# Attention: the second bank of a slot's logits for the maxima is asked for behind the filling products instead of together with the first

## The chip, the cores and the metric

One core of a Trainium2 chip runs one program: TensorE (PE, with its weight loads as PEld), VectorE (DVE), ScalarE (ACT), GpSimd (POOL) and SyncE (SP, which here issues nearly all transfers). The metric is the device time of one execution in microseconds (us). The kernel before takes 866.9 us, the median of three runs between 866.54 and 867.04.

## The reference

A transformer block on 2048 rows of 512 numbers, in float32:

```
h = layernorm(x) * (1 + ca) + sa
x = x + ga * A(h)          # attention, 32 heads of 16, 4 segments of 512 rows
h = layernorm(x) * (1 + cb) + sb
x = x + gb * ((h @ w_gate) * (h @ w_up)) @ w_down

A, per segment and head:
  p     = softmax(q k^T / 4 + mask)          # causal inside the segment
  a_dot = p v
  a_mem = phi(q) M / (phi(q) z + 1e-6)       # memory of the earlier segments
  o     = g * a_mem + (1 - g) * a_dot
  M, z += phi(k)^T v, sum phi(k)
```

The change touches how `softmax(q k^T)` is scheduled. Nothing that is computed changes.

## The kernel before

**Units.** Attention is cut into 32 units: a segment, a group of eight heads, and half of that group (four heads). A unit v runs through five slots, 0 to 4, in the loop near the end of the attention part. Each unit's logits are computed twice. First, with queries on the partitions, for the row maxima: `q_step(u, i)` (L284). It multiplies into two PSUM banks, `lq0` and `lq1`, each of which exists once, and VectorE reads each bank back with a custom masked minimum (`tensor_tensor_reduce`, shown as CUSTOM_DVE_ANT_0, followed by a short read of the accumulator) into a column of `nm`. Later, with keys on the partitions, for the exponentials: `k_step(v, slot)` (L319) multiplies into the two-bank tile `lk`, which also exists once, ScalarE takes `Exp` of both banks at once (L336), and GpSimd cuts the triangle (L342).

**What one slot contains, in program order.** The maxima's logits of a later unit (`q_step`, unit v+2 in slots 2 to 4, v+1 in slots 0 and 1); in slot 1 the products of the weights with the values of unit v-1 (`av_step`, tile `tb`, 32 products); in slot 4 the transposes of the unit before (`t_step`, tile `tr`, which VectorE turns into `rd` and `orow`); the filling products (`fill`, L1186: projections, memory products, layer norm transposes, each with their copies on ScalarE and their arithmetic on VectorE and GpSimd); and the keys' logits (`k_step`). Behind slot 2 stands `n_step(v+1)`: TensorE transposes `nm` (`ntp`), VectorE splits it into two bfloat16 rows (`nt`), and SP writes them into rows 96 and 97 of the queries, where `k_step(v+1, 0)` finds them some slots later.

**The shapes of `q_step`.** Step i = 0 and 2 (slots 2 and 4): one product of 512 columns per bank. Step 1 and 3 (slots 3 and 0): a product of 384 and one of 128 per bank. Step 4 (slot 1): two of 256 per bank.

**What sets the order.** TensorE's order is the program's: `MM` and `TP` chain every product to the one before. VectorE's order is the program's too, during attention (`vec.eng = CV`). The orders of ScalarE, GpSimd and SP are chosen by the scheduler of the framework, so they can move when the program is written in another order. A product into `lq0` or `lq1` has to wait until VectorE has reduced that bank for the last slot; one into `lk` until ScalarE has taken the exponential of the last slot.

**After attention** the feed-forward part runs with other pools; no line of it is touched.

Of the kernel before, what the change touches and what calls it, by code (L numbers as in the profile page):

```python
# [8 lines left out]
F32 = mybir.dt.float32  # L9
# [3 lines left out]
ALU = mybir.AluOpType  # L13
# [4 lines left out]
P = 128  # L18
S, D, H, DH, NSEG, L, F = 2048, 512, 32, 16, 4, 512, 1376
# [5 lines left out]
NEG = -3.0e38  # L25
# [32 lines left out]
def tile_kernel(ctx, tc, x, wq, wk_, wv, wo, beta, w_gate, w_up, w_down, c, w_mod, out):  # L58
# [4 lines left out]
    def open_pool(**kw):  # L63
        p = tc.tile_pool(**kw)
        return p, p.__enter__()
# [6 lines left out]
    def pe(i):  # L72

        if last_pe[0] is not None:
            tc.add_manual_dep(i.ins, last_pe[0].ins.name, NOSYNC, reason="order")
        last_pe[0] = i
        return i
# [6 lines left out]
    def MM(*a, **k):  # L84
        return pe(nc.tensor.matmul(*a, **k))  # L85
# [5 lines left out]
    vec, act = Switch(nc.vector), Switch(nc.scalar)  # L91
# [3 lines left out]
    psppool, psp = open_pool(name="psp", bufs=1, space=PSUM)  # L95
# [21 lines left out]
    def flush():  # L117

        while later:
            later.pop(0)()  # L120

    def rest_of():

        while soon:
            soon.pop(0)()
# [116 lines left out]
    def run(gen):  # L242
        try:
            while True:
                next(gen)
        except StopIteration as e:
            return e.value
# [10 lines left out]
    NQ = NSEG * NG * 2  # L258
    kst = [ap.tile([98, HQ, L], BF, name=f"kst{i}") for i in range(NB)]
    qst = [ap.tile([98, HQ, L], BF, name=f"qst{i}") for i in range(NB)]  # L260
    cmask = ap.tile([P, L], BF, name="cmask")
# [17 lines left out]

    nms = {}  # L280

    def q_step(u, i):

        Q, K = qst[u % NB], kst[u % NB]  # L284
        if i == 0:
            nms[u] = ap.tile([P, 16], F32, tag="nm", name=f"nm{u}", bufs=2)
        nm = nms[u]
        for b in range(2):
            h = i // 2 * 2 + b
            if i == 4:  # L290
                parts = ((2 * b, 1), (2 * b + 1, 1))
            else:
                parts = ((h, 3),) if i % 2 == 0 else ((h, 2), (h, 0))
            qp = psp.tile([P, L], F32, tag=f"lq{b}", name=f"q{u}_{i}_{b}", bufs=1)
            c = 0
            for hh, qb in parts:
                n = (qb + 1) * P
                MM(qp[:, c:c + n], Q[0:96, hh, qb * P:(qb + 1) * P], K[0:96, hh, 0:n], start=True, stop=True)
                c += n
            c = 0  # L300
            for hh, qb in parts:
                n = (qb + 1) * P
                vec.tensor_tensor_reduce(qp[:, c:c + n], qp[:, c:c + n], cmask[:, L - n:], -1.0, -NEG,
                                         ALU.add, ALU.min, nm[:, 4 * hh + qb:4 * hh + qb + 1])
                c += n

    def n_step(u):

# [37 lines left out]
    def av_step(u, kb):  # L346

        s, g, jq = u // 8, u // 2 % 4, u % 2
        if kb == 0:
            tbs[u] = pst([P, L], "tb", f"tb{u}", F32)  # L350
        n = L - kb * P
        for j in range(HQ):
            p, b = j // 2, j % 2
            hh = g * HG + jq * HQ + j
            if kb == 0:
                rhs, w = ptiles[u, p][:, b, :], sels[u, 1]
            elif kb == 2:
                rhs, w = ptiles[u, 4][:, p, 256 * b:256 * b + 256], sels[u, 4]
            else:
                c = 0 if kb == 1 else 384  # L360
                rhs, w = ptiles[u, 2 + p][:, b, c:c + n], sels[u, 3]
            x = MM(tbs[u][32 * j:32 * j + 32, kb * P:], vt[s % 2][kb][:, hh * VS:hh * VS + 32], rhs,
                   start=kb == 0, stop=kb == 2, tile_position=(0, 32 * j), skip_group_check=True)
            if j == 0:
                tc.add_manual_dep(x.ins, w.ins.name, SYNC, reason="all four heads")
        if kb == 2:
            tsbs[u] = ap.tile([P, L], F32, tag="tsb", name=f"tsb{u}", bufs=2)
            act.activation(tsbs[u], tbs.pop(u), AF.Copy)  # L368
# [140 lines left out]
    def wo_load(s, pool):  # L509
        rw = []  # L510
        for t in range(4):
            a = pool.tile([P, D], F32, tag="orl", name=f"orl{s}_{t}", bufs=4)
            n = D - P if s == NSEG - 1 else D
            pin(nc.sync.dma_start(a[:, 0:n], od[s][t][:, 0:n]))
            rw.append(a)
        return rw

    def wo_op(s, rw, us, gs=range(NG), stop=False):

        for g in gs:  # L520
            op = bank(f"op{s}_{g}", small=not stop)
            for t in range(4):
                a = rw[t][:, g * P:(g + 1) * P]
                if s == NSEG - 1 and g == NG - 1:
                    a = orows[NSEG * NG - 1][:, t].rearrange("p h e -> p (h e)")
                TP(op[:, t * P:(t + 1) * P], a, ident)
            nm = ("k", "q")[g % 2]
            i = s % 2 * 2 + g // 2
            oH = pw.tile([P, L], F32R, tag=f"w{nm}H{i}", name=f"oH{s}_{g}", bufs=1)
            oL = pw.tile([P, L], F32R, tag=f"w{nm}L{i}", name=f"oL{s}_{g}", bufs=1)  # L530
            ahead.append(act.activation(oH, op, AF.Copy))  # L531
            us.append((oH, oL))
            if stop:
                yield 0.45
                pin(vec.tensor_sub(oL, op, oH.bitcast(F32)))
            else:
                (soon if (s, g) in ((1, 0), (2, 1)) else later).append(lambda oL=oL, op=op, oH=oH: pin(vec.tensor_sub(oL, op, oH.bitcast(F32))))
                yield 0.45
            if stop and g % 2 == 1:
                yield False  # L540

    def xr_load(s, pool, tag="xr"):
        xrs = []
        for t in range(4):
            xr = pool.tile([P, D], F32, tag=tag, name=f"xr{s}_{t}", bufs=4)
            pin(nc.sync.dma_start(xr, x[rows(s, t), :]))
            xrs.append(xr)
        return xrs
# [546 lines left out]
    def until(*key):  # L1095
        while key not in done:
            credit[0] -= (mem_step() if len(key) == 3 and memq else next(fa)) or 0.0
# [52 lines left out]
    for v in range(-2, NQ + 1):  # L1150
        rate[0] = 5.5
        on, prev = 0 <= v < NQ, 0 <= v - 1 < NQ
        for slot in range(5):
            i = (slot + 3) % 5
            u = v + 2 if i < 3 else v + 1
            now[0] = slot
            if 0 <= u < NQ:
                q_step(u, i)
            if slot == 2:
                later.extend(after_n)  # L1160
                after_n.clear()
            flush()
            if prev and slot == 1:
                for kb in (0, 1, 3, 2):
                    av_step(v - 1, kb)
            if v == NQ and slot == 0:
                assert B["orl_free"]
                o3 = wo_load(3, wpool)
                xr3 = xr_load(3, B["pb"])
            if v == NQ and slot == 2:  # L1170
                for f in (fa, fb):
                    for _ in f:
                        pass
                btag[:] = ["ms", "sm", "ms"]
                us3 = []
                run(wo_op(3, o3, us3, range(NG - 1), True))
                lg1 = lnC(1, wpool, lambda: pc, wpool, "orl", 4, lambda name: dbank(name))
                next(lg1)
            if prev and slot == 4:
                if (v - 1) % 2 == 0 and v > 8:  # L1180
                    until((v - 1) // 8, (v - 1) // 2 % 4, 0)
                t_step(v - 1)
                if (v - 1) % 8 == 7:
                    osegs[0] += 1
            if slot == 2 and prev and (v - 1) % 8 == 7:
                vfree[0] = (v - 1) // 8 + 2  # L1186
            fill(share[slot], slot < 4)
            rest_of()
            if on:
                k_step(v, slot)  # L1190
            while behind:
                behind.pop(0)()
            if slot == 2 and 0 <= v + 1 < NQ:
                n_step(v + 1)
                if v + 3 < NQ:
                    load(v + 3)
            if slot == 1 and 3 <= v + 3 < NQ:
                until((v + 3) // 8, (v + 3) // 2 % 4)
# [91 lines left out]
    def dbank(name):  # L1290
        nd[0] += 1
        return pst((P, 512), ("lq0", "lk0", "lq1", "lk1")[nd[0] % 4], name)
# [310 lines left out]
    for n in range(NU):  # L1603
        p, nm, i = units[n]
# [69 lines left out]
```

## Time and profile before

| | |
|---|---|
| median of three runs | 866.9 us |
| profiled execution, its own time | 867.63 us |
| its span, first to last instruction | 865.9 us |
| attention slots, from the first exponential to the last | 55.2 to 494.5 us |
| busy: PE, DVE, ACT, POOL | 840.0, 648.3, 496.4, 273.9 us |
| granted TensorE clock, mean | 0.999 |

A timeline row gives start, duration, engine, line, operation and tiles; "x2" means that two instructions are merged into the row, and a bracket at the end gives the idle time of the engine before it and what ended it. In a row with groups the numbers behind the bar are busy us, the mean ns of one, and then the engine's idle time just before instructions of that group, with its releasers. Ends of products are modelled, so a product's row may reach beyond the start of the next one.

### The profile page before, as it was taken

The page shows a single profiled execution, that of the slowest core. Times are in us where ns is not written, and L with a number is a line of the kernel's source. Part 1 is how long each engine was busy: PE and PEld are TensorE (multiplying, and loading weights), DVE is VectorE, ACT ScalarE, POOL GpSimd, SP SyncE. Part 2 cuts the span into 40 slices and gives each one's busy share as a digit, 9 for nine tenths or more (in the row PEclk, how much of TensorE's full clock was granted, in tenths as well). Part 3 has the DMA queues.
Part 4 walks back from the last instruction along what each step waited for, and adds up shares of the span by engine and source line. Part 5 has one row for each costly group of instructions (what it writes and reads, how often), then busy time and mean ns, then how long its engine had stood idle before and what let it go on. Part 6 is the DMA issues. An engine that isn't in the chain of part 4 may idle for free.

```text
span 865.9 us, 14418 instructions
## 1 busy us (share of the span) xinstructions
PE 840.0 (97%) x4982; PEld 598.4 (69%) x4982; DVE 648.3 (75%) x1796; ACT 496.4 (57%) x759; POOL 273.9 (32%) x423
## 2 busy tenths in 40 slices
PE   9989999989999999999999999999999999999998
PEld 6755656555665656665666677788888778888876
DVE  6897767887778877688879457989987855446654
ACT  4758757677776785677545626344536546455230
POOL 2756536466546674575424610000000000000000
PEclk9999999999999999999999999999999999999999
DMA  8655434545526354557466348569561576335102
GB/s 268 141 165 146 120 102 123 154 138 157 152 76 189 112 147 123 128 157 238 127 225 195 114 160 266 207 209 341 197 232 50 196 265 213 153 134 182 32 18 97
DMA packets 83928, 139.57 MB, mean 161 GB/s; under 512 B 12720, under 2 KB 46768, under 8 KB 83856
## 3 DMA queue, kind: packets, MB, share of 16 engines
q1 hardware_dynamic: 83568, 138.52, 51.0%
q8 instruction: 39, 0.64, 0.3%
q14 instruction: 33, 0.27, 0.1%
q10 hardware_dynamic: 288, 0.15, 0.1%
HBM read 89.87 MB, written 48.50 MB: 160 GB/s over the span
## 4 chain that ended last, share of the span: by engine, by line
PE 80%; DVE 11%; ACT 6%; POOL 1%; issue 1%; DMA 1%; DVEq 0%; POOLq 0%; ACTq 0%
PE acc L1350 14%; PE tb L85 7%; PE Xg L1281 7%; PE Xu L1281 7%; PE k L85 6%; DVE q L39 6%; PE q L85 5%; PE vps L85 5%; PE wops L85 5%; PE Yu L1281 4%; PE Yg L1281 4%; PE kps L85 3%; PE qps L85 3%; ACT pt L336 2%; PE Zg L1281 1%; PE Zu L1281 1%
## 5 line engine op out<-in xcount | busy, mean ns | idle before, releaser
L39 DVE CUSTOM_DVE_ANT_0 q<-q,cmask 128x384 f32<-128x384 f32 (+3 forms) x512 | 245.6, 507 | 59.6 <-PE q L85 51.6
L336 ACT ACTIVATE pt<-k 128x1024 f32<-128x1024 f32 x160 | 163.8, 1024 | 65.0 <-PE k L85 64.6
L342 POOL TENSOR_SCALAR_AFFINE_SELECT pt<-pt 128x256 f32<-128x256 f32 (+1 forms) x224 | 97.4, 449 | 166.6 <-ACT pt L336 166.3
L85 PE MATMUL q<-kst,qst 96*128 96x384 bf16 (+3 forms) x512 | 103.3, 298 | 13.0 <-DVE nm L39 11.7
L85 PE MATMUL k<-qst,kst 98*128 98x384 bf16 (+3 forms) x512 | 97.1, 302 | 4.5 <-ACT pt L336 4.4
L1358 DVE TENSOR_TENSOR xa<-xa,acc 128x512 f32<-128x512 f32 x95 | 64.7, 682 | 39.8 <-PE acc L1350 38.0
L85 PE MATMUL tb<-pt,v 128*32 128x512 f32 (+3 forms) x1024 | 75.7, 436 | 0.0
L39 DVE DVE_READ_ACCUMULATOR2_ANT nm<- 128x1 f32 x512 | 71.7, 140 | 0.0
L85 PEld LDWEIGHTS <-kst 98*128 98x128 bf16 x512 | 37.8, 98 | 49.0 <-issue 43.0
L85 PEld LDWEIGHTS <-qst 96*128 96x128 bf16 x512 | 45.7, 97 | 35.7 <-issue 13.3
L1350 PE MATMUL acc<-dH,mH 128*128 128x512 f32 (+1 forms) x152 | 60.3, 397 | 0.0
L1350 PE MATMUL acc<-dL,mH 128*128 128x512 f32 (+1 forms) x152 | 60.1, 395 | 0.0
L1350 PE MATMUL acc<-dH,mL 128*128 128x512 f32 (+1 forms) x152 | 60.0, 394 | 0.0
L85 PEld LDWEIGHTS tb<-pt,v 128*32 128x32 f32 x1024 | 28.6, 109 | 38.8 <-issue 35.0
L368 ACT ACTIVATE tsb<-tb 128x512 f32<-128x512 f32 x32 | 19.0, 595 | 40.1 <-PE tb L85 40.1
L1350 PEld LDWEIGHTS acc<-dL,mH 128*128 128x128 f32 (+1 forms) x152 | 28.6, 188 | 7.1
L1350 PEld LDWEIGHTS acc<-dH,mL 128*128 128x128 f32 (+1 forms) x152 | 28.5, 188 | 7.1 <-DVE mL L1301 0.3
L1350 PEld LDWEIGHTS acc<-dH,mH 128*128 128x128 f32 (+1 forms) x152 | 28.5, 188 | 6.7
L85 PE MATMUL kps<-ahH,wkH 128*128 128x512 f32 x64 | 29.5, 461 | 0.0
L85 PE MATMUL wops<-woH,oH 128*128 128x512 f32 x64 | 28.2, 441 | 0.7 <-ACT oH L531 0.7
L85 PE MATMUL qps<-ahH,wqH 128*128 128x512 f32 x64 | 28.7, 448 | 0.0
L85 PE MATMUL vps<-wvH,ahH 128*128 128x512 f32 x64 | 28.3, 442 | 0.0
(399 smaller groups left out, 2021.4 us busy)
## 6 DMA issues: line engine op xcount, KB each, us to landing
wm<-in_w_mod_dram SPq DMA_DIRECT2D x24, 256.0 KB, 4.9
kd<-k SPq DMA_DIRECT2D x16, 384.0 KB, 2.9
qd<-q SPq DMA_DIRECT2D x16, 384.0 KB, 3.1
kst<-kd SPq DMA_DIRECT2D x32, 192.0 KB, 3.2
qst<-qd SPq DMA_DIRECT2D x32, 192.0 KB, 3.6
x<-in_x_dram SPq DMA_DIRECT2D x16, 256.0 KB, 4.5
kst<-kd SPq DMA_DIRECT2D x32, 128.0 KB, 3.1
qst<-qd SPq DMA_DIRECT2D x32, 128.0 KB, 3.5
```

The source lines that it names most:

```text
L39: i = getattr(self.eng, name)(*a, **k)
L85: return pe(nc.tensor.matmul(*a, **k))
L336: ex = act.activation(pt, kp, AF.Exp, scale=0.25)
L342: sels[u, i] = nc.gpsimd.affine_select(w, w, pattern=[[0, w.shape[1]], [1, P]], compare_op=ALU.is_ge, fill=0.0, base=0, channel_multiplier=-1)
L368: act.activation(tsbs[u], tbs.pop(u), AF.Copy)
L1281: pe(nc.tensor.matmul(ps[0:n], a, b[:, k], start=first and c == 0, stop=last and c == 5, skip_group_check=True))
L1350: pe(nc.tensor.matmul(ps, a[0:m, t * P:(t + 1) * P], b[0:m], start=j == 0, stop=j == n - 1))
L1358: vec.tensor_add(xa, xa, ps)
```

## The change

`q_step` becomes `q_half(u, i, b)`, which does one bank. At the head of the slot only bank 0 is asked for; bank 1 comes behind the filling products and ahead of the keys' logits.

```
-    def q_step(u, i):
+    def q_half(u, i, b):
...
-        if i == 0:
+        if i == b == 0:
             nms[u] = ap.tile([P, 16], F32, tag="nm", name=f"nm{u}", bufs=2)
...
-        for b in range(2):
-            h = i // 2 * 2 + b
...
+        h = i // 2 * 2 + b
...
             if 0 <= u < NQ:
-                q_step(u, i)
+                q_half(u, i, 0)
...
             fill(share[slot], slot < 4)
             rest_of()
+            if 0 <= u < NQ:
+                q_half(u, i, 1)
             if on:
                 k_step(v, slot)
```

No instruction is added or removed. What moves, at three places (the name q6_0_1 means unit 6, step 0, bank 1; vps are filling products for the values, k4_2 the keys' logits of unit 4 in slot 2).

TensorE in unit 4, slot 2, before:

```order
L85 LDWEIGHTS qst2_188
L85 MATMUL q6_0_0_1539<-kst2_184,qst2_188 128x512
L85 LDWEIGHTS qst2_188
L85 MATMUL q6_0_1_1542<-kst2_184,qst2_188 128x512
L85 MATMUL vps1_2_1547<-wvH0_264,ahH1_0_1066 128x512
L85 MATMUL vps1_2_1547<-wvH0_264,ahL1_0_1067 128x512
L85 MATMUL vps1_2_1547<-wvL0_265,ahH1_0_1066 128x512
L85 MATMUL vps1_2_1547<-wvH1_268,ahH1_1_1101 128x512
L85 MATMUL vps1_2_1547<-wvH1_268,ahL1_1_1102 128x512
L85 MATMUL vps1_2_1547<-wvL1_269,ahH1_1_1101 128x512
L85 LDWEIGHTS kst0_182
L85 MATMUL k4_2_1554<-qst0_186,kst0_182 128x384
```

and now:

```order
L85 LDWEIGHTS qst2_188
L85 MATMUL q6_0_0_1539<-kst2_184,qst2_188 128x512
L85 MATMUL vps1_2_1544<-wvH0_264,ahH1_0_1061 128x512
L85 MATMUL vps1_2_1544<-wvH0_264,ahL1_0_1062 128x512
L85 MATMUL vps1_2_1544<-wvL0_265,ahH1_0_1061 128x512
L85 MATMUL vps1_2_1544<-wvH1_268,ahH1_1_1098 128x512
L85 MATMUL vps1_2_1544<-wvH1_268,ahL1_1_1099 128x512
L85 MATMUL vps1_2_1544<-wvL1_269,ahH1_1_1098 128x512
L85 LDWEIGHTS qst2_188
L85 MATMUL q6_0_1_1551<-kst2_184,qst2_188 128x512
L85 LDWEIGHTS kst0_182
L85 MATMUL k4_2_1554<-qst0_186,kst0_182 128x384
```

The second bank's weight load and product went behind the six filling products; the filling products moved up by one product.

VectorE in unit 4, slot 4 (rd and orow belong to the transposes of the unit before), before:

```order
L39 ISA q6_2_0_1602,nm6_1538<-q6_2_0_1602,cmask_190 128x512
L39 ISA nm6_1538 128x1
L39 ISA q6_2_1_1605,nm6_1538<-q6_2_1_1605,cmask_190 128x512
L39 ISA nm6_1538 128x1
L39 RECIPROCAL rd3_1613<-tr3_1608 128x16
L39 TENSOR_TENSOR orow1_1452<-tr3_1608,rd3_1613 128x4x64
L39 ISA q6_3_0_1632,nm6_1538<-q6_3_0_1632,cmask_190 128x384
```

and now:

```order
L39 ISA q6_2_0_1602,nm6_1538<-q6_2_0_1602,cmask_190 128x512
L39 ISA nm6_1538 128x1
L39 RECIPROCAL rd3_1610<-tr3_1605 128x16
L39 TENSOR_TENSOR orow1_1449<-tr3_1605,rd3_1610 128x4x64
L39 ISA q6_2_1_1621,nm6_1538<-q6_2_1_1621,cmask_190 128x512
L39 ISA nm6_1538 128x1
L39 ISA q6_3_0_1632,nm6_1538<-q6_3_0_1632,cmask_190 128x384
```

The slot's other VectorE work now stands ahead of the second bank's reduction.

ScalarE in unit 7, slots 2 and 3 (pt7_2 and pt7_3 are the exponentials of these slots; kf, k3, rlk and phk work up a projection of the keys that a filling product has finished), before:

```order
L820 ACTIVATE kf1_2_2084<-kps1_2_1991 128x512
L336 ACTIVATE pt7_2_2099<-k7_2_2094 128x1024
L824 ACTIVATE k3_1_2_2086<-kf1_2_2084 128x512
L848 ACTIVATE rlk1_2_2091<-kf1_2_2084 128x512
L848 ACTIVATE phk1_2_2090<-kf1_2_2084 128x512
L907 ACTIVATE us1_1_2076<-up1_1_1_2126 128x272
L336 ACTIVATE pt7_3_2143<-k7_3_2138 128x1024
```

and now:

```order
L819 ACTIVATE kf1_2_2081<-kps1_2_1988 128x512
L823 ACTIVATE k3_1_2_2083<-kf1_2_2081 128x512
L847 ACTIVATE rlk1_2_2088<-kf1_2_2081 128x512
L847 ACTIVATE phk1_2_2087<-kf1_2_2081 128x512
L335 ACTIVATE pt7_2_2099<-k7_2_2094 128x1024
L906 ACTIVATE us1_1_2073<-up1_1_1_2121 128x272
L827 CAST k3_1_2_2083<-kr_1_2_2084 128x512
```

The scheduler put the exponential of slot 2 behind the three copies that had followed it. The same happens at ten exponentials of the 160: at pt2_3, pt6_3, pt7_2, pt8_3, pt10_3, pt11_2, pt15_3, pt16_2, pt19_3 and pt23_3. Other single swaps on ScalarE, GpSimd and SP are there too, none of them by more than two places.

More of the change, by code (lines that the diff above doesn't have):

```diff
@@ L280, in tile_kernel @@
     nms = {}
-    def q_step(u, i):
+    def q_half(u, i, b):
         Q, K = qst[u % NB], kst[u % NB]
-        if i == 0:
+        if i == b == 0:
             nms[u] = ap.tile([P, 16], F32, tag="nm", name=f"nm{u}", bufs=2)
         nm = nms[u]
-        for b in range(2):
-            h = i // 2 * 2 + b
[L290 to L305, printed above, removed]
+        h = i // 2 * 2 + b
+        if i == 4:
+            parts = ((2 * b, 1), (2 * b + 1, 1))
+        else:
+            parts = ((h, 3),) if i % 2 == 0 else ((h, 2), (h, 0))
+        qp = psp.tile([P, L], F32, tag=f"lq{b}", name=f"q{u}_{i}_{b}", bufs=1)
+        c = 0
+        for hh, qb in parts:
+            n = (qb + 1) * P
+            MM(qp[:, c:c + n], Q[0:96, hh, qb * P:(qb + 1) * P], K[0:96, hh, 0:n], start=True, stop=True)
+            c += n
+        c = 0
+        for hh, qb in parts:
+            n = (qb + 1) * P
+            vec.tensor_tensor_reduce(qp[:, c:c + n], qp[:, c:c + n], cmask[:, L - n:], -1.0, -NEG,
+                                     ALU.add, ALU.min, nm[:, 4 * hh + qb:4 * hh + qb + 1])
+            c += n
     def n_step(u):
```

## The prediction

> **What bounds the kernel now.** I read the page's busy shares first, then the table of busy time by stretch, then the groups of TensorE rows with shapes kept apart, then single slots in the timeline, and the chain of waits between them.
>
> ```profile
> PE 840.0 (97%) x4982; PEld 598.4 (69%) x4982; DVE 648.3 (75%) x1796; ACT 496.4 (57%) x759; POOL 273.9 (32%) x423
> 200.00:250.00 50.00, 49.40 (x347) 32.30 (x345) 39.24 (x140) 33.84 (x47) 26.36 (x40) 1.00 0.46 124
> 550.00:600.00 50.00, 50.00 (x217) 40.49 (x217) 46.39 (x86) 22.45 (x41) 0.00 (x0) 1.00 0.70 244
> L85 PE MATMUL q<-kst,qst 96*128 96x512 bf16 x128 | 42.6, 379 | 7.2 <-DVE nm L39 7.0
> L85 PE MATMUL q<-kst,qst 96*128 96x384 bf16 x128 | 35.2, 326 | 0.4 <-DVE nm L39 0.4
> L85 PE MATMUL q<-kst,qst 96*128 96x256 bf16 x128 | 21.8, 271 | 5.3 <-DVE nm L39 4.2 <-DVE den L39 0.5
>   DVE nm L39: 11.7, 30
>   DVE den L39: 0.5, 1
> ```
>
> In the two rows of stretches the columns behind the length are PE, PEld, DVE, ACT, POOL. TensorE is the bound in both stages; the feed-forward stretch has no idle at all, so what attention gains or loses passes through to the end. In attention (200 to 250) VectorE is busy 39.2 of 50 and ScalarE 33.8: neither is the bound on average, both are close enough to be late in single slots. The waits that the change can touch are the next three rows: 7.2 us ahead of the 512-column products (slots 2 and 4), 5.3 ahead of the 256-column ones (slot 1), 0.4 ahead of the others, 12.9 in all, in some 31 waits.
>
> These 12.9 are too few. One regular stretch of unit 4, VectorE and then TensorE:
>
> ```profile
> 112.92 0.70 DVE L39 CUSTOM_DVE_ANT_0 q<-q,cmask 128x512 f32<-128x512 f32 x1 [1.34 <-PE q L85]
> ...
> 113.54 0.73 DVE L39 CUSTOM_DVE_ANT_0 q<-q,cmask 128x512 f32<-128x512 f32 x1
> 114.19 0.14 DVE L39 DVE_READ_ACCUMULATOR2_ANT nm<- 128x1 f32 x1
> 115.10 0.28 DVE L39 CAST nt<-ntp 16x128 bf16<-16x128 f32 x1 [0.77 <-PE ntp L88]
> ...
> 115.63 0.54 DVE L39 CUSTOM_DVE_ANT_0 q<-q,cmask 128x384 f32<-128x384 f32 x1
> ...
> 116.48 0.60 DVE L39 CUSTOM_DVE_ANT_0 q<-q,cmask 128x384 f32<-128x384 f32 x1
> ...
> 117.39 0.14 DVE L39 DVE_READ_ACCUMULATOR2_ANT nm<- 128x1 f32 x1
> ...
> 112.50 0.60 PE L85 MATMUL q<-kst,qst 96*128 96x512 bf16 x2
> ...
> 114.34 0.61 PE L85 MATMUL k<-qst,kst 98*128 98x384 bf16 x4
> 114.79 0.28 PE L88 MATMUL ntp<-ident,nm 128*16 128x128 f32 x1
> 114.90 0.60 PE L85 MATMUL q<-kst,qst 96*128 96x384 bf16 x4
> ...
> 116.79 0.61 PE L85 MATMUL k<-qst,kst 98*128 98x384 bf16 x4
> 117.24 0.72 PE L85 MATMUL q<-kst,qst 96*128 96x512 bf16 x2
> 117.80 0.38 PE L88 MATMUL tr<-ident,tsb 128*128 128x128 f32 x2
> ```
>
> Two undisturbed 512-column products make a row of 0.60 (112.50); at 117.24 the same two make 0.72, with no idle shown. The second one did wait 0.12, because VectorE finished the second bank of slot 3 only at 117.53 (117.39 + 0.14); the wait is swallowed by the modelled end of the first (0.38 mean, of which 0.60 - 0.38 = 0.22 is the real pitch). So each wait that is shown is short by about 0.16, and those under 0.16 don't show. With 31 waits that is 12.9 + 5.0 = 17.9 at most; I take **17 us** as what TensorE loses to these waits, split like the shown idle: 9.5 at 512 columns, 7.0 at 256, 0.5 at the rest. The Trainium skill (Perfetto Trace Analysis, section Tensor Engine Instruction) says that a product's reported end is an estimate from its size and not observed; the trace agrees with the 0.72 against 0.60. Taken without that, the sum would start from 12.9.
>
> **The change, part by part.** No product, reduction or transfer is added: 160 weight-and-product groups move within a slot, and every wait on a bank stays, only at another place.
>
> *Seams.* Before, a slot has one passage from filling products to bfloat16 logits (filling to k) and one back (q to filling). It still has one of each (filling to second q, first q to filling): 0.
>
> *Slot 3 into slot 4 (most of the 9.5).* Before, VectorE has to do nt and both banks of slot 3 before TensorE can go past the second product of slot 4: 115.63 to 117.53 is 1.90 for the banks. Now the second product of slot 2 stands ahead of k: at 114.34 - 0.22 = 114.1 (the filling products came up by 0.22, the k logits stay). Its reduction takes 0.42 to start (112.50 to 112.92) and lasts 0.79 (113.54 to 114.33), to 115.3. nt follows, 0.53, to 115.8 instead of 115.63; then one bank of slot 3, 0.95, to 116.8. That is what the first product of slot 4 needs at 117.24: 0.4 to spare where 0.12 was missing. So waits up to about 0.5 vanish and longer ones shrink by that much. Bounds: all 9.5 gone, or only the short half of them. The long ones have other VectorE work ahead of nt, which stays. I take two thirds: **-6.3** (between -4 and -9.5).
>
> *Slot 0 into slot 1 (the 7.0).* Here the chain of waits shows what is late:
>
> ```profile
> 90.37 0.48 ACT kf L820
> 90.86 1.02 ACT pt L336
> 91.88 0.52 ACT k L824
> 92.40 0.52 ACT rlk L848
> 92.92 0.53 ACT phk L848
> 93.47 0.92 DVE phk L39
> 94.39 0.47 DVE q L39
> 95.31 0.46 DVE q L39
> ```
>
> A finished projection goes through kf, an exponential, k3, rlk and phk on ScalarE, then phk on VectorE; both banks of slot 0 stand behind it (94.39 to about 96.2). Now phk is followed by the second bank of slot 4 and the first bank of slot 0: again two reductions, 0.79 + 0.95 against 1.9, and wanted 0.22 earlier, by the first product of slot 1 instead of the second. That is no relief at all. The gain is only that phk comes earlier: by 0.22, since the filling products ended earlier, and by an exponential (1.02) at places where the exponential now stands behind it. Bounds 0 and -7.0; I take a third, **-2.3**.
>
> *The exponentials.* ScalarE's order moved with the program. Unit 7:
>
> ```profile
> 157.21 0.40 PE L85 MATMUL kps<-ahL,wkH 128*128 128x512 f32 x1
> 157.44 0.61 PE L85 MATMUL k<-qst,kst 98*128 98x384 bf16 x4
> 159.66 0.61 PE L85 MATMUL k<-qst,kst 98*128 98x384 bf16 x4
> 157.64 0.60 ACT L820 ACTIVATE kf<-kps 128x512 f32<-128x512 f32 x1 [0.30 <-PE kps L85]
> 158.13 1.02 ACT L336 ACTIVATE pt<-k 128x1024 f32<-128x1024 f32 x1
> 159.03 0.63 ACT L824 ACTIVATE k<-kf 128x512 bf16<-128x512 f32 x1
> 159.56 0.63 ACT L848 ACTIVATE rlk<-kf 128x512 f32<-128x512 f32 x1
> 160.08 0.63 ACT L848 ACTIVATE phk<-kf 128x512 f32<-128x512 f32 x1
> 160.60 0.39 ACT L907 ACTIVATE us<-up 128x272 f32<-128x272 f32 x1
> 160.87 1.03 ACT L336 ACTIVATE pt<-k 128x1024 f32<-128x1024 f32 x1
> ```
>
> Now kf starts at 157.64 - 0.22 = 157.42; k3, rlk and phk follow at 0.49 and then 0.52 each, so the exponential starts at 159.47 instead of 158.13 and ends at 160.4. The next keys' logits, due at 159.66 into the same tile, wait about **0.8**. Three of the ten moved exponentials stand ahead of slot 3 (pt7_2, pt11_2, pt16_2). From k to k that slot lasted 2.22 here (157.44 to 159.66), but 2.45 with six filling products (114.34 to 116.79), so at the other two I put 0.5. The seven others stand ahead of slot 4, longer by the four transposes (two make the row at 117.80, 0.38): 0 to 0.4, and 0.25 as a rule. Sum 0.8 + 2 x 0.5 + 7 x 0.25 = **+3.5**. Bounds: 0, where VectorE's lateness covers it, and ten times 0.8. The ScalarE queue is what hurts here: the row at 160.87 shows an exponential that starts 1.21 after its first product (159.66), right behind the us that precedes it. The Trainium skill (TensorE: Matmul & The Clock Gate, section on the array being 16 pieces of 32x32) gives the queues of ScalarE and VectorE as strictly first in, first out; the trace agrees with that 1.21, and by the rule each of the ten waits for all three copies, ready or not. It is the mechanism of the slower rival below.
>
> *New waits.* The second product, and k behind it, now stand behind whatever the slot's VectorE work delays. The bank has a whole slot for that, so I price it from 0 to one reduction (0.79) at four places, 3: **+0.5**. nt is 0.2 later than before; the transfer that follows is wanted in slot 0 of the next unit, two slots of 2.4 and 2.8 later: 0. SP's loads behind it are wanted a unit later: 0.
>
> Sum: -6.3 - 2.3 + 3.5 + 0.5 = **-4.6**. The profiled execution is 867.63 (span 865.9 and 1.7 around it), 0.7 above the median of the runs; 866.9 - 4.6 = **862.3 us**.
>
> **The rivals.**
>
> *The exponentials decide (slower).* At all ten places the next keys' logits wait 0.8, +8, because the products ahead of them no longer wait for VectorE and so arrive sooner at `lk`; the relief of slot 4 is at its lower bound, -4, and slot 1 gives nothing: +4, **870.9**. For it: the rows above, where 1.34 us of delay meet a slack of 0.54. Against it: seven of the ten stand ahead of a long slot, and the phk that goes first is the one that slot 1 waits for. It decides once the exponentials cost more than slot 4 gives.
>
> *The waits move and nothing is left.* VectorE does the same reductions in the same pairs, only 0.2 to 0.8 earlier in a slot, and wants them 0.2 earlier; as in slot 1, slot 4 gets no more than the 0.12 of the regular slots, 0.12 at half of the 32 units, 1.9, and the exponentials take it: **866.9**. For it: phk, not the banks, is what is late at 93.47. Against it: 115.63 to 117.53, where nothing but the two banks is late.
>
> *Nearly all goes.* The 9.5 vanish, the early phk takes most of the 7.0 (-5), and the exponentials cost 2 where VectorE was late anyway: -12.5, **854.4**. For it: VectorE has 11 of 50 us idle. Against it: the waits of over 0.5 hang on ScalarE.
>
> **How the numbers follow.** The forecast, a gain of 2 to 9 us, has 0.52; nearly all gone 0.12; nothing left 0.12; slower 0.24. What a measurement can tell from no change is 0.2%, 1.7 us. Faster is 0.52 + 0.12 = 0.64, same 0.12, slower 0.24. The likeliest case's own range is 858 to 865; to leave out no more than two in ten I go down into the fastest case, 855, and up to the slower one, 871.
>
> **What would show it.** Right: the idle ahead of the 512-column products falls from 7.2 to 2 or less, the one ahead of the 256-column products stays above 3, and the idle ahead of k, fed by ScalarE, grows by about 3. The pair at 112.50 comes apart, and the row 117.24 has no hidden wait. Wrong: the 512-column products still wait for nm; or the keys' logits wait over 8 us for the exponential; or filling products begin to wait for VectorE, which no row here shows and for which I have no price.

## The result, and the profile after

The changed kernel takes 860.26 us (median of six runs, 859.71 to 862.23) against 866.96 us for the kernel before on the same chip (six runs): a ratio of 0.9926, 95% interval 0.9913 to 0.9938. It is faster by 6.7 us; 862.3 was forecast. Its profiled execution was its longest, 862.23 us with a span of 860.5: in it the granted clock stood at 0.50 from 137.35 to 140.76, right after TensorE's longest wait in the attention slots (1.64 us, ended at 136.49). The 32 `tb` products there took 3.75 us; 32 of them at 209.01 took 2.36. Half of 3.41 us is about 1.7 us, an estimate of what this cost; the other five runs had mean clocks of 0.999 to 1.0.

First the TensorE groups with shapes kept apart, after (behind the last bar stands the idle time just before a group and what ended it; other groups stand between these rows). The exponential, L336 before, is L335 now, and L343 in one experiment:

```profile
L85 PE MATMUL q<-kst,qst 96*128 96x512 bf16 x128 | 49.2, 384 | 2.7 <-DVE nm L39 1.5 <-DMA qd<-q 0.5
L85 PE MATMUL q<-kst,qst 96*128 96x384 bf16 x128 | 42.4, 331 | 3.3 <-DVE nm L39 3.2
L85 PE MATMUL q<-kst,qst 96*128 96x256 bf16 x128 | 24.8, 275 | 1.6 <-DVE nm L39 1.2
L85 PE MATMUL k<-qst,kst 98*128 98x512 bf16 x128 | 38.2, 379 | 0.6 <-ACT pt L335 0.6
L85 PE MATMUL k<-qst,kst 98*128 98x384 bf16 x128 | 34.9, 326 | 2.5 <-ACT pt L335 2.3
L85 PE MATMUL k<-qst,kst 98*128 98x256 bf16 x128 | 19.2, 271 | 2.6 <-ACT pt L335 2.4
```

and the keys' logits in the kernel before:

```profile
L85 PE MATMUL k<-qst,kst 98*128 98x512 bf16 x128 | 38.6, 383 | 1.8 <-ACT pt L336 1.8
L85 PE MATMUL k<-qst,kst 98*128 98x384 bf16 x128 | 35.4, 330 | 2.6 <-ACT pt L336 2.6
L85 PE MATMUL k<-qst,kst 98*128 98x256 bf16 x128 | 19.5, 275 | 0.1
```

The idle time ahead of q, most of it waits for VectorE, fell at 512 and at 256 columns, from 7.2 and 5.3 to 2.7 and 1.6, and rose at 384, from 0.4 to 3.3. The idle time ahead of k, nearly all of it waits for ScalarE's exponentials, moved: at 512 columns down by 1.2, at 256 columns up by 2.5.

Idle time is too small a number here, because a product's modelled end covers the first 0.16 us of every wait. So I also took the starts of the products: start to start, less the tenth percentile of the same pair of neighbours in the same trace, everything over 0.06 us summed from the first of the maxima's products (at 36.6 us) to the end of the attention slots. By that measure TensorE lost 22.0 us ahead of q and 5.2 ahead of k before, and 12.5 and 8.9 after. The sum fell from 27.2 to 21.4, 5.8 us. The two profiled executions differ by 867.63 - 862.23 = 5.4, or about 7.1 without the stretch at half clock, and the medians by 6.7. The table under the experiments has the same numbers for all of them, and what the measure leaves out stands below it.

The regular stretch of unit 4 that the prediction worked through, after the change:

```profile
113.97 0.70 DVE L39 CUSTOM_DVE_ANT_0 q<-q,cmask 128x512 f32<-128x512 f32 x1 [0.62 <-PE q L85]
...
114.58 0.27 DVE L39 CAST nt<-ntp 16x128 bf16<-16x128 f32 x1
...
115.10 0.54 DVE L39 CUSTOM_DVE_ANT_0 q<-q,cmask 128x384 f32<-128x384 f32 x1
...
115.95 0.14 DVE L39 DVE_READ_ACCUMULATOR2_ANT nm<- 128x1 f32 x1
116.42 0.57 DVE L39 CUSTOM_DVE_ANT_0 q<-q,cmask 128x384 f32<-128x384 f32 x1 [0.33 <-PE q L85]
...
113.54 0.39 PE L85 MATMUL q<-kst,qst 96*128 96x512 bf16 x1
...
114.32 0.38 PE L85 MATMUL q<-kst,qst 96*128 96x384 bf16 x2
...
115.99 0.39 PE L85 MATMUL q<-kst,qst 96*128 96x384 bf16 x2
...
116.66 0.38 PE L85 MATMUL q<-kst,qst 96*128 96x512 bf16 x1
```

nt now runs right behind the second bank of slot 2, one bank of slot 3 is reduced by 116.09 (115.95 + 0.14), and the first product of slot 4, at 116.66, finds it free with 0.6 to spare. Before, the second product of that slot was 0.12 late.

And ScalarE with TensorE in unit 10, at one of the ten moved exponentials, after the change:

```profile
203.15 0.60 ACT L819 ACTIVATE kf<-kps 128x512 f32<-128x512 f32 x1 [0.94 <-PE kps L85]
203.78 0.63 ACT L823 ACTIVATE k<-kf 128x512 bf16<-128x512 f32 x1
204.31 0.62 ACT L847 ACTIVATE rlk<-kf 128x512 f32<-128x512 f32 x1
204.84 0.61 ACT L847 ACTIVATE phk<-kf 128x512 f32<-128x512 f32 x1
205.35 1.00 ACT L335 ACTIVATE pt<-k 128x1024 f32<-128x1024 f32 x1
...
203.18 0.60 PE L85 MATMUL k<-qst,kst 98*128 98x384 bf16 x4
...
206.41 0.60 PE L85 MATMUL k<-qst,kst 98*128 98x256 bf16 x4 [0.34 <-ACT pt L335]
```

The logits of slot 3 were begun at 203.18, their exponential starts 2.2 us later, behind three copies, and the logits of slot 4 wait for it.

### The profile page after: what moved, and what is told of

The parts are those of the page before. It is cut to its first block, busy times and chain, and to the rows that moved or that the text cites. A ratio compares the mean times of both kernels' runs of the same rounds, so it can differ in the third digit from the quotient of the medians.

```text
span 860.5 us, 14421 instructions
## 1 busy us (share of the span) xinstructions
PE 839.1 (98%) x4982; PEld 599.1 (70%) x4982; DVE 643.1 (75%) x1796; ACT 499.1 (58%) x759; POOL 275.8 (32%) x423
## 4 chain that ended last, share of the span: by engine, by line
PE 84%; ACT 7%; DVE 6%; issue 1%; POOL 0%; DMA 0%; DVEq 0%; ACTq 0%
PE acc L1351 14%; PE tb L85 8%; PE Xg L1282 7%; PE Xu L1282 7%; PE k L85 6%; PE q L85 6%; PE wops L85 5%; PE vps L85 5%; PE kps L85 4%; PE Yu L1282 4%; PE Yg L1282 4%; DVE q L39 3%; PE qps L85 3%; ACT pt L335 2%; PE Zg L1282 1%; PE Zu L1282 1%
## 5 line engine op out<-in xcount | busy, mean ns | idle before, releaser
L335 ACT ACTIVATE pt<-k 128x1024 f32<-128x1024 f32 x160 | 163.9, 1024 | 76.9 <-PE k L85 75.0
L85 PE MATMUL q<-kst,qst 96*128 96x384 bf16 (+3 forms) x512 | 123.0, 302 | 7.6 <-DVE nm L39 6.0
L85 PEld LDWEIGHTS <-kst 98*128 98x128 bf16 x512 | 44.5, 97 | 30.2 <-issue 15.2
```

The source lines that it names most:

```text
L335: ex = act.activation(pt, kp, AF.Exp, scale=0.25)
```

## The experiments

**1. The change with the exponentials put back.** At the ten places the copies are tied behind the exponential; the order on TensorE and VectorE is that of the change. The trace shows that the scheduler answered with a move of its own: three other exponentials (pt3_0, pt8_0 and pt16_4), which stand ahead of three copies both before and in the change, come behind them here.

```
...
+        for c in copies[TEN[u, i]] if (u, i) in TEN else ():
+            tc.add_manual_dep(c.ins, ex.ins.name, NOSYNC, reason="order")
```

> The changed kernel, with the exponential put back ahead of the copies (k3 or q3, rl, ph) at the ten places where the scheduler had moved it behind them. My theory: relief of the waits on VectorE and the late exponentials are two effects that add up; the changed kernel waits some 5.9 us ahead of the keys' logits at the ten places (0.3 to 1.0 each, from its timeline), and these go, of which up to 2 come back ahead of the 256-column products, because phk is later again: 855 to 858 us. Rival: the early phk is what the change lives on; then the waits of slot 1 come back in full and the time is 861 to 866.

862.02 us, ratio 0.9950 (0.9936 to 0.9963): slower than the change by 1.8 us (only the change's longest run, the one with the stretch at half clock, reaches into the range of these), not faster by 2 to 5. The waits ahead of k did fall, from 8.9 to 3.8 us, and those ahead of q rose by more, from 12.5 to 18.9. The place is visible in unit 10, VectorE and then TensorE:

```profile
205.23 0.98 DVE L39 SCALAR_TENSOR_TENSOR phk<-phk,rlk 128x512 f32<-128x512 f32 x1 [0.82 <-ACT phk L850]
206.13 0.68 DVE L39 CUSTOM_DVE_ANT_0 q<-q,cmask 128x512 f32<-128x512 f32 x1
...
206.74 0.59 DVE L39 CUSTOM_DVE_ANT_0 q<-q,cmask 128x384 f32<-128x384 f32 x1
...
204.47 0.39 PE L85 MATMUL q<-kst,qst 96*128 96x512 bf16 x1
...
206.93 0.38 PE L85 MATMUL q<-kst,qst 96*128 96x384 bf16 x2 [0.42 <-DVE nm L39]
```

The second bank of slot 4 was written at 204.47. VectorE had nothing else to do, stood 0.82 us in front of phk waiting for ScalarE, and reduced the bank only at 206.13; the second product of slot 0 wants that bank and waits until 206.93. So the rival held in its number and in its mechanism, that the early phk pays for the late exponentials, but not in its place: in slot 1 the waits came back by 2.5 of 5.9, and as much more, 3.5, came at the 384-column products. How much of the 1.8 us the three other exponentials make, this run does not separate.

**2. The kernel before with the exponentials late.** Only ScalarE's order is changed, at the same ten places.

```
...
+        if (u, i) in TEN:
+            tc.add_manual_dep(ex.ins, copies[TEN[u, i]].ins.name, NOSYNC, reason="order")
```

> The kernel before (both banks together), with the exponential put behind the third copy at the same ten places. My theory: the exponentials come late there too, and only the part of the waits on VectorE that hangs on phk is given back: 867 to 872 us. Rival (the change lives on the early phk): 861 to 864 with both banks still together.

868.10 us, ratio 1.0013 (1.0004 to 1.0022), inside the range of the theory and outside the rival's. ScalarE's new order alone is worth nothing, rather a loss of 1.1 us: waits ahead of k rise by 6.6, those ahead of q fall by 5.4. The split without the ten (experiment 1 against before, with its three other late exponentials) is worth 5.0 us, both together 6.7.

**3 and 4. The second bank late in some slots only:** in 1 and 4, or, with (0, 2, 3) in both lines, in the others.

```
+                if slot not in (1, 4):
+                    q_half(u, i, 1)
...
-            if 0 <= u < NQ:
+            if 0 <= u < NQ and slot in (1, 4):
                 q_half(u, i, 1)
```

> Second bank behind the filling products in slots 1 and 4 alone, together with the first in slots 0, 2 and 3; the ten exponentials then stand where they stood before the change. My theory: a wait of slot 4 is a wait of its second product for the second bank of slot 3 (and slot 1 for slot 0); moving these two alone is enough, and the early reductions of slots 0, 2 and 3 keep VectorE ahead: 855 to 859 us, idle ahead of the 512- and 256-column products under 3 us together, idle ahead of k as before (4.5). Rival (spreading in every slot is what helps): two fifths of the gain, 863 to 865.

> The opposite: second bank behind the filling products in slots 0, 2 and 3, together with the first in slots 1 and 4. My theory: now the second product of slots 4 and 1 wants a bank that was handed to VectorE only some 0.7 to 0.9 us earlier, while a reduction takes about 0.4 to start and 0.8 to 1.0 to run: 0.4 to 0.7 us lost at each of 64 places, and the ten exponentials stay late: 885 to 905 us. Rival (spreading helps slot by slot): between the two kernels, 862 to 866.

Slots 1 and 4: 897.38 us, ratio 1.0348 (1.0331 to 1.0365), both theories wrong. Slots 0, 2 and 3: 912.94 us, 1.0531 (1.0517 to 1.0545), somewhat beyond my range. What I had counted for the second variant holds for the first as well: wherever a slot with a late second bank is followed by one with an early second bank, the bank is asked for twice within one k and one q. Both variants have two such passages in a unit. Slot 1 into slot 2 of a unit, TensorE and then VectorE, with late banks in slots 1 and 4:

```profile
117.34 0.39 PE L85 MATMUL q<-kst,qst 96*128 96x256 bf16 x2
...
118.01 0.38 PE L85 MATMUL q<-kst,qst 96*128 96x512 bf16 x1
118.84 0.38 PE L85 MATMUL q<-kst,qst 96*128 96x512 bf16 x1 [0.45 <-DVE nm L39]
...
117.77 0.43 DVE L39 CUSTOM_DVE_ANT_0 q<-q,cmask 128x256 f32<-128x256 f32 x1 [1.60 <-PE q L85]
...
118.65 0.14 DVE L39 DVE_READ_ACCUMULATOR2_ANT nm<- 128x1 f32 x1
```

The bank is written at 117.34, freed at 118.79, and wanted at 118.01 + 0.22. By the starts, the passage from slot 1 to slot 2 loses about 0.62 us in 31 of the 32 units, and the one from slot 4 to slot 0 loses 30 us in all. Over the two kernels that is (897.4 - 867.0) / 64 = 0.47 and (912.9 - 867.0) / 64 = 0.72 us a passage, net of all else; in it are two and three stretches of 3.41 us with a granted clock of 0.50, by the estimate above some 3.4 and 5.1 us. So the split helps only where every slot has it; the share of single slots can't be had this way.

**5 to 7. phk behind the second bank.** `feature2`, which puts phk (and phq, the same for a projection of the queries) on VectorE, is held back until the second bank's reduction has been issued; in the kernel before, until the filling products are done. `release` issues what is held back.

```
-                later.append(feature2)
+                (later if fast else heldback).append(feature2)
...
                 q_half(u, i, 1)
+            release()
```

> The changed kernel, with phk (and phq) of a filling projection put behind the second bank's reduction on VectorE instead of ahead of it; ScalarE's order stays. My theory now: what is left of the waits on VectorE is the second bank (and the first bank behind it) standing behind a phk that ScalarE has not delivered; about half of the 12 us that the starts of the products still show goes: 854 to 858 us, the 3.3 of idle ahead of the 384-column products falls under 1. Rival: the work is late by its amount and not by its place; then the wait only moves to the next bank and the time is 859.5 to 861.

> The same move in the kernel before: phk behind the filling products' other VectorE work, both banks still together at the head of the slot, ScalarE's order as before. My theory: there both banks of the slot stand ahead of phk already, and the two of the next slot behind it as before; phk is ready at the latest by then, so little changes: 865.5 to 868 us. Rival (a late phk alone is the whole matter, the split does nothing): as fast as the changed kernel with the same move, under 861.

> The changed kernel with both: the ten exponentials ahead of the copies, and phk behind the second bank's reduction. My theory: the trade between late exponentials and a late phk is undone, so the waits ahead of k fall by the 5 us that the exponentials alone gave back and the waits on VectorE do not rise again: 852 to 857 us, the fastest of all. Rival: phk is then so late that the memory products wait for it, or the next slot's first bank does: 859 to 863.

On the change: 858.66 us, ratio 0.9900 (0.9885 to 0.9916), between the two ranges, nearer to the theory's 858 than to the rival's 859.5; the 384-column idle fell from 3.3 to 1.2, not under 1. On the kernel before: 866.18 us, 0.9992 (0.9984 to 1.0001), as expected; there the edit moves hardly anything (phk or phq at four places, by one or two). On the change with the exponentials first: **856.41 us**, 0.9875 (0.9862 to 0.9889), in its range and the fastest of all, 10.6 us under the kernel before and 3.9 under the change. The three other exponentials of experiment 1 stand in their old place here. Against experiment 5 the waits ahead of k fell by 5.9, and those ahead of q rose by 3.1, which the expectation had not foreseen. Its groups on TensorE:

```profile
L85 PE MATMUL q<-kst,qst 96*128 96x512 bf16 x128 | 49.2, 384 | 4.2 <-DVE nm L39 3.4 <-DMA qd<-q 0.5
L85 PE MATMUL q<-kst,qst 96*128 96x384 bf16 x128 | 42.4, 331 | 1.3 <-DVE nm L39 1.2
L85 PE MATMUL q<-kst,qst 96*128 96x256 bf16 x128 | 24.6, 273 | 3.1 <-DVE nm L39 2.8
L85 PE MATMUL k<-qst,kst 98*128 98x384 bf16 x128 | 34.9, 326 | 0.6 <-ACT pt L343 0.3
```

and the row of VectorE's waits for phk (us in all, how many, the longest), from experiment 1 and from this kernel:

```profile
DVE phk L39 <- ACT phk L850: 8.1, 8, 2.4
...
DVE phk L39 <- ACT phk L857: 2.5, 3, 1.1
```

In experiment 5, with the ten exponentials still late, the row has 2.6 in 3 waits. Putting the exponentials first costs 1.8 us while phk stands ahead of the bank (with three others late), and brings 2.3 us (858.66 to 856.41) once it stands behind it.

All of them by the starts of the products, in us (medians, waits lost ahead of q by columns, and ahead of k):

| | median | q 512 | q 384 | q 256 | k |
|---|---|---|---|---|---|
| before | 867.0 | 12.2 | 1.0 | 8.7 | 5.2 |
| the change | 860.3 | 5.3 | 4.4 | 2.8 | 8.9 |
| 1: exponentials put back | 862.0 | 5.8 | 7.9 | 5.3 | 3.8 |
| 2: before, exponentials late | 868.1 | 10.4 | 1.2 | 4.9 | 11.8 |
| 5: phk behind | 858.7 | 5.8 | 1.8 | 3.0 | 9.3 |
| 6: before, phk behind | 866.2 | 12.2 | 1.1 | 7.8 | 5.3 |
| 7: phk behind, exponentials first | 856.4 | 6.9 | 2.1 | 4.7 | 3.4 |

The measure misses waits at pairs of neighbours that occur once or twice, since such a pair has no start that did not wait to be compared with. In the kernel before two long waits ahead of k fall out so (at 188.82 and 328.53, 0.7 and 0.8 us). Where a pair occurs fewer than four times, one can take the tenth percentile of all products behind the same neighbour instead. Then q and k lose 22.4 and 8.1 us before, 14.3 and 9.5 in the change, and the sum falls by 6.7; in experiments 1, 5, 6 and 7 it falls by 5.4, 8.3, 0.9 and 10.9, and in experiment 2 it rises by 1.1. The medians fell by 6.7, by 5.0, 8.3, 0.8 and 10.6, and rose by 1.1.

## Why the prediction held, and where its terms were off

**What TensorE loses at the start.** I took 17 us, 9.5, 7.0 and 0.5 by width. The starts give 22.0: 12.2, 8.7 and 1.0. The correction of the shown 12.9 was right in its kind and too small in its count: 63 of these products start over 0.06 us late, not 31. The 40 that show idle time show 0.16 too little on average, as the prediction had it; the other 23, 2.8 us together, show none.

**Slot 3 into slot 4, -6.3.** Right: the 512-column waits fell by 6.9 (by 6.4 with the rare pairs), and the stretch of unit 4 has the spare that was worked out (0.6 for 0.4).

**Slot 0 into slot 1, -2.3.** Too small: -5.9. That this slot waits for phk was right. That the split alone gives no more than phk's 0.22 us fits and is not shown: with the exponentials put back the term is -3.4, and 22 waits of this kind times 0.22 would be 4.8. The other 2.5 of the 5.9 come from ScalarE's new order. Both parts were priced too low.

**The exponentials, +3.5.** At k the rise is 3.7 by the table, 1.4 with the rare pairs, and 1.2 in shown idle. That is a net figure: what the ten late exponentials cost at k is what experiment 1 gives back, 5.1 (8.9 to 3.8), so the term was priced too low and the split's own relief at k was not seen. Nor are they a loss of the change: with the exponentials put back the kernel is 1.8 slower. The prediction counted the early phk only in slot 1 and not for the second bank.

**New waits, +0.5.** This is the term that was mis-sized: the second bank stands behind phk on VectorE, and the next slot's second product behind it, +3.4 at 384 columns in the change and +6.9 with the exponentials put back. The prediction said that "the bank has a whole slot for that"; unit 10 of experiment 1 shows that a phk waiting for ScalarE uses the slot up. In the change itself the longest wait is of this kind:

```profile
134.25 1.52 DVE L39 SCALAR_TENSOR_TENSOR phk<-phk,rlk 128x512 f32<-128x512 f32 x1 [2.36 <-ACT phk L847]
135.69 0.69 DVE L39 CUSTOM_DVE_ANT_0 q<-q,cmask 128x512 f32<-128x512 f32 x1
...
136.49 0.38 PE L85 MATMUL q<-kst,qst 96*128 96x384 bf16 x2 [1.64 <-DVE nm L39]
```

This 1.64 is half of the 3.3 of idle at 384 columns. Another 1.01, at 54.94, stands behind a layer norm's statistics on VectorE and stays in experiments 5 and 7.

**The signs foretold.** None of the three numbers came out: "2 or less" at 512 columns was 2.7, "above 3" at 256 was 1.6, and k's shown idle rose by 1.2 in place of 3 (3.7 by the starts). The pair at 112.50 did come apart, and the hidden wait of 117.24 is gone. Of the signs of being wrong, the 512-column products still wait for nm, 1.5 us in place of 7.0, and the keys' logits wait 8.9 us by the starts, over the 8 that was named, but 5.7 in shown idle; filling products show as little idle as before. The slower rival, with the exponentials deciding, needed them to cost more than slot 4 gives; they cost 5.1 against 6.9.

Terms off by +2.9 and -3.6 nearly cancelled. That the sum, -4.6, came closer to the -6.7 than its parts did was luck.

Still open is why the split gains 5.0 us in experiment 1: its waits fell by 4.4 in total, which fits, but no run separates the reductions' new places from the filling products' 0.22, nor from the three exponentials that are late there alone.

## What to carry to other kernels

On an engine that works in program order, ask of every instruction not how long it takes but whom it waits for and who stands behind it: moving one instruction that waits for a third engine behind work that is ready gave 1.6 us here, and with it in place the exponentials put first, which had lost 1.8 (with three others late), brought 2.3. When a buffer is asked for at a later point of a cycle, do it in every round of the cycle; a late request followed by an early one cost 0.5 to 0.7 us on average, net of all else. And after reordering one engine's program, compare the orders of the engines that the scheduler fills in: two effects of one edit can lie there, and an edit that puts ten instructions back can move three others, as in experiment 1.

## What was not expected of the hardware

Waits of TensorE that leave no idle time in the profile: of the 27.2 us that the starts of these products give before the change, the rows show 12.9 + 4.5 = 17.4 us. And the length of one VectorE instruction on a 128x512 tile, phk, depends on when it runs: 0.68 to 0.98 us within the few rows of unit 10 in the two kernels. Why was not tried, but the traces of before, the change and experiments 1, 5 and 7 hold a hint: of the 120 executions of phk and phq, the 13 with no GpSimd row beside them took 0.68 to 0.69 us, and every longer one ran beside GpSimd, such as the 1.52 at 134.25. That is not shown to be the cause, as some beside GpSimd took 0.68 too (the one at 205.53 in the change).

The granted clock halved, to 0.50 for 3.41 us, after TensorE had stood idle for 1.64 us in the profiled execution of the change (at 137.35). After 1.63 us at the same place in experiment 1 (ended at 135.63) it did not, nor after 2.21 us in experiment 3 (ended at 142.87). What decides was not tried.
